# Moving the w2 load to another queue, and reordering norms, key finals and z sums in a linear-attention block

## Chip, cores and metric

The kernel runs on one core of one Trainium2 chip. The metric is the device time of one execution in microseconds (us). The profile is one execution; its span (239.8 us) is a little shorter than the timed runs, since it counts from the first to the last recorded instruction.

## What is computed

The input is x with 2048 rows (tokens) of 640 elements, in bf16. The reference, cut to what matters:

```python
xn  = (x - mean(x)) / sqrt(var(x) + 1e-5)              # per row
qkv = xn @ wqkv                                        # 640 -> 3 * 640, 32 heads of 20
phi = lambda t: where(t > 0, t + 1, exp(t)) + 1e-6
pq, pk = phi(q), phi(k)
kv  = sum over rows of pk^T v                          # per head, 20 x 20
z   = sum over rows of pk                              # per head, 20
o   = (pq @ kv) / (pq . z + 1e-6)
s   = o @ wo                                           # 640 -> 640
g   = silu(relu(xn @ w1) @ w2)                         # 640 -> 1728 -> 640
out = x + s * g
```

## The kernel before

The program is written as one list of operations. A small scheduler gives each engine its part of the list, in the order of the list, and puts semaphore waits in front of an operation for what it reads and overwrites. So an engine never overtakes in its own list, and neither does a queue of transfers: the order in the text is the order on each engine.

The 2048 tokens are 16 tiles of 128 (t), or four chunks of 512 (j). The stages follow each other on TensorE:

1. tiles 0 to 3: transposed on TensorE, keys K (L471);
2. chunks 0 to 3: H blocks (w1, 13 of 128 columns for each chunk, L546), Q blocks (L524) and the K of the other tiles, in the order of a plan;
3. the denominators, then G = xn^T pk (160 matmuls, L759);
4. for eight pairs of tiles: U = hT w2 (L811), between them kv (L774), W = kv wo (L788) and the output tiles s (L850).

VectorE computes the statistics of a tile (L394, L398), GpSimd its reciprocal root (L400, L402), VectorE the normed tile (L413). A DMA transpose (L462) makes it an operand for K, H and Q.

```python
def aggr(t):                                   # VectorE L398, then GpSimd L400, L402
    bn_aggr(mv[:, t], stats[:, t])             # DVE
    rsv[:, t] = mv[:, t, 1] + EPS_LN           # POOL
    rsy[:, t] = rsv[:, t] ** -0.5              # POOL

def LN_stats(t): bn(t, 0); bn(t, 1); aggr(t)   # bn: DVE L394

def LN_norm(t):                                # DVE L413
    xn[:, t, :] = (xin[:, t % XR, :] - mv[:, t, 0:1]) * rsy[:, t:t + 1]
    if t + XR < T: x_load(t + XR)

def K_mm(t, b, ...):                           # PE L471, 10 matmuls of 128x320
def K_exp(t, b), K_relu(t, b):                 # ACT L488
def K_fin(t):                                  # DVE L504, L506
    e_ = min(e_, 1.0) + 1e-6
    pk[:, t, :] = e_ + r_
    zpend.append(t)

def z_add():                                   # POOL L482
    t = zpend.pop(0)
    zacc = zacc + pk[:, t, :]                  # fp32 accumulator, 128x640

def Q_block(j, f):                             # PE L524, 5 matmuls of 128x512, a bank of a ring of six
    e_ = exp(ps[b])                            # ACT L531
    r_ = max(ps[b], 0) + 1e-6                  # DVE L532, waits for the exp
    pqT[:, f, schunk(j)] = min(e_, 1) + r_     # DVE L534

def H_block(j, f):                             # PE L546, 5 matmuls of 128x512, a bank of the same ring
    hT[:, f, schunk(j)] = relu(ps[b])          # ACT L550
```

The plan of the chunks. Chunk 0 has 13 H blocks; chunk 1 has ten Q blocks between them, chunks 2 and 3 five each. `kat` says after which step of the plan the keys of a tile follow, `lnat` after which its statistics.

```python
for j in range(J):
    for n, item in enumerate(plans[j]):
        Q_block(...) or H_block(...)
        if n in lnat[j]:
            t = lnat[j][n]
            LN_stats(t)
            if j == 0:
                K_fin(t - 4); LN_norm(t); xnT_dma(t); LN_norm(t - 4); xnT_dma(t - 4)
        if j > 0 and n - 1 in lnat[j]:
            LN_norm(lnat[j][n - 1]); xnT_dma(lnat[j][n - 1])
        if n in kat[j]:
            K_mm(t, 0); K_exp(t, 0); K_relu(t, 0); K_fin(t)
        if n >= 3 and zpend and len(zpend) > (1 if j < J - 1 else 0):
            z_add()
        ...
        if j == J - 1:                         # the last chunk
            if n == 2:  z_split()              # POOL
            if n == 8:  z_col()                # PE, DVE
            if n == 14: H_half(0); H_half(1); den()
```

The end of `den` and what follows it on SyncE's queue:

```python
    # den(): PE L651, then DVE L656 and the reciprocal L660
    for i in range(J):                         # L666: reciprocals, repeated 20 times, to scratch memory
        dma("SP", scr[...] <- rden[...], R=[("rden",)], W=[("scr", i)])
    for m in range(C):                         # L672: read back into the layout of pqT
        dma("SP", Rr[m] <- scr[P*m : P*(m+1), :], R=[("scr", i) for i in range(J)], W=[("Rr", m)], ...)

for a in range(2):                             # L742: w2 takes the place of w1, so it waits for the last w1 matmul
    dma("SP", w2_sb[...] <- B_w2[...], W=[("w2", a)], extra=[lastW1])
for u in range(2):                             # L746
    dma("SP", w2l[...] <- B_w2[NF*P:FF, :], W=[("w2l", u)], extra=[lastW1])
for c in range(VC):                            # L750: takes the place of the tiles of x
    dma("SP", wo_sb[:, c, :] <- A_wo[...], W=[("wo", c)], extra=[last_norm[0]])
for jx in range(4):                            # L883: x once more, for the last sum
    dma("SP", xre[...] <- x2[...], W=[("xre", jx)], extra=[lastG])

def divide(i):                                 # DVE L677, five of them for each chunk
    pqT[:, m, schunk(i)] *= Rr[m][:, schunk(i)]
```

U of a tile is four groups of 13 matmuls for a pair (L811). In the stage U the operations `kv_block` and `divide` follow the first group, the W blocks the groups of pair 1, the output tiles the groups from pair 2 on.

Of the kernel before, what the change touches and what calls it, by code (L numbers as in the profile page):

```python
# [214 lines left out]
def bass_recurrent_scan__linear_attn_block__dense_activation_relu__prompt_kernel(  # L215
# [9 lines left out]
    Bb, S, D = A_x.shape  # L225
# [3 lines left out]
    FF = B_w1.shape[1]  # L229
    P = 128  # L230
    T = S // P
    J = S // 512
    C = D // P
    NF = FF // P
# [102 lines left out]
    def x_load(t):  # L337
        sl = t % XR
        dma("SP", lambda eng: eng.dma_start(xin[:, sl, :], x2[tok(t), :]), W=[("xin", sl)])

    def w_load(dst, src, key, extra=(), E="SP"):
        dma(E, lambda eng: eng.dma_start(dst, src.rearrange("(c p) n -> p c n", p=P)), W=[key], extra=extra)

    KA = 3
    F1 = 7 * P
    x_load(0)
    x_load(1)
    w_load(wqk[:, 0:KA, D:2 * D], A_wqkv[0:KA * P, D:2 * D], ("wk", 0))
    x_load(2)
    w_load(wqk[:, KA:C, D:2 * D], A_wqkv[KA * P:D, D:2 * D], ("wk", 1))  # L350
    x_load(3)
    w_load(w1_sb[:, :, 0:F1], B_w1[:, 0:F1], ("w1", 0))
    for t in range(4, XR):
# [9 lines left out]
    sc.op("POOL", lambda eng: eng.memset(mhalf[:, :], -0.5), W=[("mhalf",)])  # L363
    sc.op("POOL", lambda eng: eng.memset(ones[:, :], 1.0), W=[("ones",)])
    sc.op("POOL", lambda eng: eng.memset(zacc[:, :], 0.0), W=[("zacc",)])
    NWARM = 28
    sc.group("PE", [(lambda eng: eng.matmul(ps[7][:, 0:P], lhsT=zero[:], rhs=zero[:], start=True, stop=True))
                    for _ in range(NWARM)], R=[("zero",)], W=[("ps", 7)])
    sc.allow_unread.add(("ps", 7))

    def build_consts():
        sc.op("POOL", lambda eng: eng.memset(mh[:, :, :], 1.0), W=[("mh",)])
# [19 lines left out]
    def bn(t, a):  # L392
        xv = xin[:, t % XR, :]
        sc.op("DVE", lambda eng: eng.bn_stats(stats[:, t, a, :], xv[:, HN * a:HN * (a + 1)]),  # L394
              R=[("xin", t % XR)], W=[("stats", t, a)])
# [16 lines left out]
    def LN_norm(t):  # L412
        last_norm[0] = sc.op("DVE", lambda eng: eng.tensor_scalar(  # L413
            out=xn[:, t, :], in0=xin[:, t % XR, :], scalar1=mv[:, t, 0:1], scalar2=rsy[:, t:t + 1],
            op0=ALU.subtract, op1=ALU.mult), R=[("xin", t % XR), ("mv", t), ("rsy", t)], W=[("xn", t)])
        if t + XR < T:
            x_load(t + XR)
# [6 lines left out]
    def mean_act(t, lo):  # L424
        junk = ek[:, t % NEK, 0, 0:D - lo]
        sc.op("ACT", lambda eng: eng.activation(out=junk, in_=xin[:, t % XR, lo:D], func=ACTF.Copy, scale=1.0 / D,
                                                accum_out=msum[:, t, 1:2]),
              R=[("xin", t % XR)], W=[("msum", t, 1), ("ek_e", t % NEK)])
        sc.allow_unread.add(("ek_e", t % NEK))

    def centre(t):
        if t == 0:
            sc.op("DVE", lambda eng: eng.tensor_scalar(
                out=xn[:, t, :], in0=xin[:, t, :], scalar1=msum[:, t, 0:1], scalar2=msum[:, t, 1:2],
                op0=ALU.subtract, op1=ALU.subtract), R=[("xin", t), ("msum", t, 0), ("msum", t, 1)], W=[("xn", t)])
        else:
            sc.op("DVE", lambda eng: eng.tensor_scalar(
                out=xn[:, t, :], in0=xin[:, t, :], scalar1=msum[:, t, 1:2], scalar2=None,
                op0=ALU.subtract), R=[("xin", t), ("msum", t, 1)], W=[("xn", t)])
# [10 lines left out]
    def xcT_copy(t, b, part):  # L450
        psb = ps[b + part].bitcast(bf)
        c0, c1 = (0, TS) if part == 0 else (TS, C)
        dst = xcT[:, c0:c1, tok(t)]
        src = psb[:, 0:P * (c1 - c0)].rearrange("p (c q) -> p c q", c=c1 - c0)
        if part == 0:
            sc.op("DVE", lambda eng: eng.tensor_copy(dst, src), R=[("ps", b)], W=[("xcT", t, 0)])
        else:
            sc.op("ACT", lambda eng: eng.activation(out=dst, in_=src, func=ACTF.Copy), R=[("ps", b + 1)],
                  W=[("xcT", t, 1)])

    def xnT_dma(t):
        dma("SP", lambda eng: eng.dma_start_transpose(xnT[:, :, tok(t)], xn[:, t, :]), R=[("xn", t)], W=[("xnT", t)])  # L462
# [3 lines left out]
    def K_mm(t, b, k0=0, k1=C, halves=(0, 1)):  # L466
        fns = []
        for a in halves:
            for k in range(k0, k1):
                lhs = xcT if t < 4 else xnT  # L470
                fns.append(lambda eng, a=a, k=k, lhs=lhs: eng.matmul(  # L471
                    ps[b + a][:, 0:HN], lhsT=lhs[:, k, tok(t)], rhs=wqk[:, k, D + HN * a:D + HN * (a + 1)],
                    start=(k == 0), stop=(k == C - 1)))
        Rx = [("xnT", t)] if t >= 4 else ([("xcT", t, 0)] if k0 < TS else []) + ([("xcT", t, 1)] if k1 > TS else [])
        Rw = ([("wk", 0)] if k0 < KA else []) + ([("wk", 1)] if k1 > KA else [])
        sc.group("PE", fns, R=Rx + Rw, W=[("ps", b + a) for a in halves])
# [23 lines left out]
    def K_fin(t):  # L500
        es = t % NEK
        e_ = ek[:, es, 0, :]
        r_ = ek[:, es, 1, :]
        sc.op("DVE", lambda eng: eng.tensor_scalar(out=e_, in0=e_, scalar1=1.0, scalar2=1e-6, op0=ALU.min, op1=ALU.add),  # L504
              R=[("ek_e", es)], W=[("ek_e", es)])
        sc.op("DVE", lambda eng: eng.tensor_tensor(out=pk[:, t, :], in0=e_, in1=r_, op=ALU.add),  # L506
              R=[("ek_e", es), ("ek_r", es)], W=[("pk", t)])
        zpend.append(t)
# [65 lines left out]
    mean_act(0, HN)  # L574
    half_mean_dve()
    centre(0)
    mean_act(1, 0)
    transposes(0, 0)
    xcT_copy(0, 0, 0)
    xcT_copy(0, 0, 1)  # L580
    centre(1)
    K_mm(0, 2, 0, TS)
    bn(0, 1)
    aggr(0)
    mean_act(2, 0)
    K_mm(0, 2, TS, KA)
    transposes(1, 6)
    xcT_copy(1, 6, 0)
    xcT_copy(1, 6, 1)
    centre(2)  # L590
    K_mm(0, 2, KA, C)
    mean_act(3, 0)
    K_mm(1, 4, 0, TS)
    K_mm(1, 4, TS, C, (0,))
    transposes(2, 0)
    bn(1, 0)
    xcT_copy(2, 0, 0)
    xcT_copy(2, 0, 1)
    K_mm(1, 4, TS, C, (1,))
    w_load(w1_sb[:, :, F1:FF], B_w1[:, F1:FF], ("w1", 1), E="ACT")  # L600
    K_exp(0, 2)
    K_relu(0, 2)
    centre(3)
    bn(1, 1)
    aggr(1)
    K_mm(2, 6, 0, TS)
# [86 lines left out]
            if ql:  # L693
                plans[j].append(("q",) + ql.pop(0))
    kat = [{5: 4, 7: 5, 9: 6, 11: 7}, {7: 8, 11: 9, 15: 10, 19: 11}, {6: 12, 9: 13, 12: 14, 15: 15}, {}]
    lnat = [{0: 4, 2: 5, 4: 6, 6: 7}, {0: 8, 4: 9, 8: 10, 12: 11}, {0: 12, 3: 13, 6: 14, 9: 15}, {}]
    for j in range(J):
        for n, item in enumerate(plans[j]):
            if item[0] == "q":
                Q_block(item[1], item[2])  # L700
            else:
                lastW1 = H_block(item[1], item[2])
            if n in lnat[j]:
                t = lnat[j][n]
                LN_stats(t)
                if j == 0:
                    K_fin(t - 4)
                    LN_norm(t)
                    xnT_dma(t)
                    LN_norm(t - 4)  # L710
                    xnT_dma(t - 4)
            if j > 0 and n - 1 in lnat[j]:
                t = lnat[j][n - 1]
                LN_norm(t)
                xnT_dma(t)
            if n in kat[j]:
                t = kat[j][n]
                K_mm(t, 0)
                K_exp(t, 0)
                K_relu(t, 0)  # L720
                K_fin(t)
            if n >= 3 and zpend and len(zpend) > (1 if j < J - 1 else 0):
                z_add()
            if j == 1 and n == 2:
                w_load(wv_sb[:, :, :], A_wqkv[:, 2 * D:3 * D], ("wv",))
            if j == 2 and n == 1:
                build_consts()
            if j == J - 1:
                while zpend:
                    z_add()  # L730
                if n == 2:
                    z_split()
                if n == 8:
                    z_col()
                if n == 14:
                    lastW1 = H_half(0)
                    lastW1 = H_half(1)
                    den()

    for a in range(2):  # L740
        c0, c1 = (0, 7) if a == 0 else (7, NF)
        dma("SP", lambda eng, c0=c0, c1=c1: eng.dma_start(  # L742
            w2_sb[:, c0:c1, :], B_w2[P * c0:P * c1, :].rearrange("(c p) n -> p c n", p=P)),
            W=[("w2", a)], extra=[lastW1])
    for u in range(2):
        dma("SP", lambda eng, u=u: eng.dma_start(w2l[64 * u:64 * (u + 1), :], B_w2[NF * P:FF, :]),  # L746
            W=[("w2l", u)], extra=[lastW1])
    for c in range(VC):
        r0 = VR * c if c < VC - 1 else D - P
        dma("SP", lambda eng, c=c, r0=r0: eng.dma_start(wo_sb[:, c, :], A_wo[r0:r0 + P, :]),  # L750
            W=[("wo", c)], extra=[last_norm[0]])

    def G_block(k, b):
# [208 lines left out]
```

## Time and profile before

The median of three timed runs is 240.54 us (240.16 to 243.49).

| engine | busy us | share of the span |
|---|---|---|
| TensorE, matmuls (PE) | 219.2 | 91% |
| TensorE, weight loads (PEld, beside the matmuls) | 134.0 | 56% |
| VectorE (DVE) | 112.5 | 47% |
| ScalarE (ACT) | 87.8 | 37% |
| GpSimd (POOL) | 45.0 | 19% |

The stretches of the old kernel, from the view of busy times by window:

| stretch, us | what | PE busy | DVE busy | POOL busy | DMA share, GB/s |
|---|---|---|---|---|---|
| 0 to 15.2 | loads, tiles 0 to 3 | 11.85 | 7.04 | 3.79 | 0.81, 267 |
| 15.2 to 37.5 | chunk 0 | 19.57 | 18.65 | 14.30 | 0.69, 169 |
| 37.5 to 67.8 | chunk 1 | 30.14 | 27.01 | 9.34 | 0.21, 50 |
| 67.8 to 94.0 | chunk 2 | 25.10 | 17.50 | 10.78 | 0.13, 26 |
| 94.0 to 117.1 | chunk 3, denominators | 22.84 | 10.20 | 3.49 | 0.00, 1 |
| 117.1 to 139.1 | G | 21.94 | 1.00 | 0.00 | 0.78, 212 |
| 139.1 to 148.6 | between G and U | 0.05 | 0.00 | 3.30 | 1.06, 359 |
| 148.6 to 239.8 | U, kv, W, s | 87.69 | 31.12 | 0.00 | 0.19, 64 |

How to read the profile: a line such as "L482" is a line of the kernel's source. A row of groups gives line, engine, operation, output<-input, the count, the busy time and the mean of one in ns. A row of waits reads "who waited <- for whom: us in total, times, the longest". A row of the timeline is start, length, engine, line, operation, count, and in brackets the idle time before it with what ended it; a row may merge several like instructions. In the page's slices each digit is the busy share of one fortieth of the span in tenths; PEclk is the clock that TensorE was granted.

### The profile page before, as it was taken

To read this page: it belongs to the slowest core of one execution; us is meant where nothing else is said; L and a number is where in the kernel's file an instruction comes from. 1 tells how busy PE (TensorE), PEld (TensorE's weight loads), DVE (VectorE), ACT (ScalarE), POOL (GpSimd) and SP (SyncE) were. 2 spreads that over 40 slices of the span, in tenths; PEclk is the share of its full clock that TensorE was granted. 3 is DMA by queue.
4 is the path that set the end of the run, shared out by engine and by line. 5 is a ranking of instruction groups with operands and counts; after the bars stand their busy time and mean duration, and the time that the engine had idled before them with its cause. 6 is when DMAs were issued, how large, how long until landed. Compare 5 with 4: busy or idle time off the path is not lost.

```text
span 239.8 us, 3474 instructions
## 1 busy us (share of the span) xinstructions
PE 219.2 (91%) x1425; PEld 134.0 (56%) x1436; DVE 112.5 (47%) x211; ACT 87.8 (37%) x144; POOL 45.0 (19%) x69
## 2 busy tenths in 40 slices
PE   6899969999999989999999912999999999999994
PEld 5554434555545544444577701767776776777672
DVE  3388995999847981560600000482132432224143
ACT  5496635566655655554212130023202110210211
POOL 2154673333241365200000050000000000000000
PEclk9999999999999999999999995799999999999998
DMA  6998740511101120000099799920010101000011
GB/s 190 353 296 178 165 113 12 164 29 27 31 0 27 30 52 3 0 0 3 15 211 211 262 386 338 363 79 0 3 55 27 57 27 55 30 27 29 28 55 56
DMA packets 26992, 23.90 MB, mean 100 GB/s; under 512 B 11744, under 2 KB 26336, under 8 KB 26976
## 3 DMA queue, kind: packets, MB, share of 16 engines
q1 hardware_dynamic: 25664, 21.80, 31.2%
q10 hardware_dynamic: 1312, 1.88, 2.4%
q8 instruction: 11, 0.18, 0.3%
q14 instruction: 5, 0.04, 0.1%
HBM read 15.81 MB, written 5.24 MB: 88 GB/s over the span
## 4 chain that ended last, share of the span: by engine, by line
PE 64%; DMA 14%; DVE 13%; SPq 3%; POOL 2%; issue 2%; ACT 1%; DVEq 0%
PE psT L811 25%; PE psT L546 13%; PE psT L850 8%; PE psT L524 8%; PE psT L471 6%; DMA reg<-in_B_w_dram 5%; DMA scr<-regE 4%; DVE reg L413 3%; DVE stats L394 3%; DMA reg<-reg 2%; DMA reg<-in_A_wqkv_dram 2%; POOL rsy L402 2%; DVE pqT L534 2%; SPq L666 1%; DVE regE L660 1%
## 5 line engine op out<-in xcount | busy, mean ns | idle before, releaser
L811 PE MATMUL psT<-reg,hT 128*128 128x320 bf16 x416 | 62.2, 304 | 9.5 <-DMA reg<-in_B_w_dram 9.5
L811 PEld LDWEIGHTS psT<-reg,hT 128*128 128x128 bf16 x416 | 40.8, 99 | 27.1 <-issue 10.9
L546 PE MATMUL psT<-reg 128*128 128x512 bf16 x191 | 45.5, 379 | 0.3 <-issue 0.2
L550 ACT ACTIVATE hT<-psT 128x512 bf16<-128x512 f32 x52 | 30.9, 600 | 18.3 <-PE psT L546 18.3
L864 DVE TENSOR_TENSOR reg<-psT,reg 128x640 bf16<-128x640 f32 (+1 forms) x17 | 13.3, 785 | 48.8 <-PE psT L850 47.6
L546 PEld LDWEIGHTS psT<-reg 128*128 128x128 bf16 x195 | 19.0, 98 | 22.1 <-ACT hTl L567 0.4
L482 POOL TENSOR_TENSOR zacc<-zacc,reg 128x640 f32<-128x640 f32 x16 | 23.0, 1435 | 7.9 <-DVE reg L506 7.6
L850 PE MATMUL psT<-reg,pqT 128*128 128x320 bf16 x160 | 24.3, 299 | 0.0
L524 PE MATMUL psT<-reg 128*128 128x512 bf16 x95 | 23.8, 379 | 0.3
L839 ACT ACTIVATE reg<-psT 128x640 bf16<-128x640 f32 x12 | 8.2, 702 | 43.1 <-PE psT L811 23.6
L759 PE MATMUL psT<-reg 128*128 128x320 bf16 x160 | 21.9, 299 | 0.0
L471 PE MATMUL psT<-reg 128*128 128x320 bf16 x120 | 18.3, 299 | 3.6 <-DMA reg<-reg 2.9
L488 ACT ACTIVATE regE<-psT 128x640 bf16<-128x640 f32 x24 | 15.6, 701 | 13.4 <-PE psT L471 13.4
L759 PEld LDWEIGHTS psT<-reg 128*128 128x128 bf16 x160 | 15.7, 98 | 6.2
L850 PEld LDWEIGHTS psT<-reg,pqT 128*128 128x128 bf16 x160 | 15.7, 98 | 6.1
L532 DVE TENSOR_SCALAR regE<-psT 128x512 bf16<-128x512 f32 x20 | 13.6, 680 | 11.3 <-ACT regE L531 11.3
L413 DVE TENSOR_SCALAR reg<-reg,mv,rsy 128x640 bf16<-128x640 bf16 x16 | 16.5, 1051 | 3.3 <-POOL rsy L402 3.3
L777 DVE TENSOR_TENSOR reg<-psT,mv 128x120 bf16<-128x120 f32 (+1 forms) x6 | 1.5, 268 | 34.8 <-PE psT L774 34.8
L471 PEld LDWEIGHTS psT<-reg 128*128 128x128 bf16 x120 | 11.3, 97 | 11.2 <-ACT hT L550 3.0
L839 ACT ACTIVATE reg<-psT,rsy 128x640 bf16<-128x640 f32 x4 | 3.2, 794 | 35.3 <-PE psT L829 30.1
L524 PEld LDWEIGHTS psT<-reg 128*128 128x128 bf16 x100 | 9.7, 98 | 11.4
L534 DVE SCALAR_TENSOR_TENSOR pqT<-regE 128x512 bf16<-128x512 bf16 x20 | 15.3, 766 | 0.7
(68 smaller groups left out, 175.8 us busy)
## 6 DMA issues: line engine op xcount, KB each, us to landing
reg<-in_A_x_dram SPq DMA_DIRECT2D x16, 160.0 KB, 2.8
scr<-regE SPq DMA_DIRECT2D x4, 640.0 KB, 8.7
reg<-in_A_x_dram SPq DMA_DIRECT2D x4, 640.0 KB, 10.6
out_dram<-reg SPq DMA_DIRECT2D x15, 160.0 KB, 1.8
reg<-in_B_w_dram SPq DMA_DIRECT2D x2, 1120.0 KB, 9.1
regE<-scr SPq DMA_DIRECT2D x4, 512.0 KB, 5.2
reg<-in_B_w_dram ACTq DMA_DIRECT2D x1, 1040.0 KB, 5.2
reg<-in_B_w_dram SPq DMA_DIRECT2D x1, 960.0 KB, 13.2
```

Of the source, the lines that this page charges most:

```text
L413: last_norm[0] = sc.op("DVE", lambda eng: eng.tensor_scalar(out=xn[:, t, :], in0=xin[:, t % XR, :], scalar1=mv[:, t, 0:1], scalar2=rsy[:, ...
L471: fns.append(lambda eng, a=a, k=k, lhs=lhs: eng.matmul(ps[b + a][:, 0:HN], lhsT=lhs[:, k, tok(t)], rhs=wqk[:, k, D + HN * a:D + HN * (a + 1)],
L482: sc.op("POOL", lambda eng: eng.tensor_tensor(out=zacc[:, :], in0=zacc[:, :], in1=pk[:, t, :], op=ALU.add), R=[("zacc",), ("pk", t)], W=[( ...
L488: sc.op("ACT", lambda eng: eng.activation(out=o_.rearrange("p (a n) -> p a n", a=2), in_=ps2(b, HN), func=func, scale=scale), R=[("ps", b) ...
L524: sc.group("PE", [(lambda eng, k=k: eng.matmul(ps[b], lhsT=wqk[:, k, P * f:P * (f + 1)], rhs=xnT[:, k, schunk(j)], start=(k == 0), stop=(k ...
L532: sc.op("DVE", lambda eng: eng.tensor_scalar(out=r_, in0=ps[b], scalar1=0.0, scalar2=1e-6, op0=ALU.max, op1=ALU.add), R=[("ps", b), ("er_e ...
L534: sc.op("DVE", lambda eng: eng.scalar_tensor_tensor(out=pqT[:, f, schunk(j)], in0=e_, scalar=1.0, in1=r_, op0=ALU.min, op1=ALU.add), R=[(" ...
L546: a = sc.group("PE", [(lambda eng, k=k: eng.matmul(ps[b], lhsT=w1_sb[:, k, P * f:P * (f + 1)], rhs=src[:, k, :], start=(k == 0), stop=(k = ...
L550: sc.op("ACT", lambda eng: eng.activation(out=hT[:, f, schunk(j)], in_=ps[b], func=ACTF.Relu), R=[("ps", b)], W=[("hT", j, f)])
L759: fns.append(lambda eng, t=t, a=a: eng.matmul(ps[b + a][:, 0:HN], lhsT=xn[:, t, P * k:P * (k + 1)], rhs=pk[:, t, HN * a:HN * (a + 1)], sta ...
L811: sc.group("PE", [(lambda eng, f=f: eng.matmul(ps[b][:, 0:HN], lhsT=hT[:, f, tok(t)], rhs=w2_sb[:, f, HN * n:HN * (n + 1)], start=(f == 0 ...
L850: sc.group("PE", [(lambda eng, c=c, a=a: eng.matmul(ps[b + a][:, 0:HN], lhsT=pqT[:, c, tok(t)], rhs=wf[:, c, HN * a:HN * (a + 1)], start=( ...
```

## The change

Five things are altered, in the order of the program.

1. The first loads: the key weights wk come ahead of the second tile of x, in pieces of two and three blocks (KA = 2 where it was 3). The warm-up matmuls of zeros are 32 where they were 28, six more stand behind the first transposes, and the sums, centrings and statistics of tiles 0 to 3 take other places in the list. It is to start the first keys sooner.
2. Chunk 0: the statistics and norms of tiles 4 to 7 come at steps 0 to 3, ahead of the finals of the keys of tiles 0 to 3; the norms and transposes of tiles 0 to 3 come after them. It is to have the transposed tiles ready for K.
3. In chunks 1 and 2 the norms come closer together. The z adds begin at a late step of each chunk (`zfrom`): none in chunk 0, from step 10 in chunk 1, from step 8 in chunk 2. It is to keep GpSimd's adds apart from the norms on VectorE.
4. Chunk 3: wo is loaded at its first step, z_split, z_col and the denominators come at steps 1, 6 and 11 where they came at 2, 8 and 14.
5. w2 is loaded from ScalarE's queue, where it stood on SyncE's behind the writes and reads of scr. It is to arrive before U needs it.

The diff:

```diff
--- before.py
+++ after.py
@@ -341,13 +341,13 @@
     def w_load(dst, src, key, extra=(), E="SP"):
         dma(E, lambda eng: eng.dma_start(dst, src.rearrange("(c p) n -> p c n", p=P)), W=[key], extra=extra)
 
-    KA = 3
+    KA = 2
     F1 = 7 * P
     x_load(0)
+    w_load(wqk[:, 0:KA, D:2 * D], A_wqkv[0:KA * P, D:2 * D], ("wk", 0))
     x_load(1)
-    w_load(wqk[:, 0:KA, D:2 * D], A_wqkv[0:KA * P, D:2 * D], ("wk", 0))
+    w_load(wqk[:, KA:C, D:2 * D], A_wqkv[KA * P:D, D:2 * D], ("wk", 1))
     x_load(2)
-    w_load(wqk[:, KA:C, D:2 * D], A_wqkv[KA * P:D, D:2 * D], ("wk", 1))
     x_load(3)
     w_load(w1_sb[:, :, 0:F1], B_w1[:, 0:F1], ("w1", 0))
     for t in range(4, XR):
@@ -363,10 +363,13 @@
     sc.op("POOL", lambda eng: eng.memset(mhalf[:, :], -0.5), W=[("mhalf",)])
     sc.op("POOL", lambda eng: eng.memset(ones[:, :], 1.0), W=[("ones",)])
     sc.op("POOL", lambda eng: eng.memset(zacc[:, :], 0.0), W=[("zacc",)])
-    NWARM = 28
-    sc.group("PE", [(lambda eng: eng.matmul(ps[7][:, 0:P], lhsT=zero[:], rhs=zero[:], start=True, stop=True))
-                    for _ in range(NWARM)], R=[("zero",)], W=[("ps", 7)])
+
+    def fill(n):
+        sc.group("PE", [(lambda eng: eng.matmul(ps[7][:, 0:P], lhsT=zero[:], rhs=zero[:], start=True, stop=True))
+                        for _ in range(n)], R=[("zero",)], W=[("ps", 7)])
+
     sc.allow_unread.add(("ps", 7))
+    fill(32)
 
     def build_consts():
         sc.op("POOL", lambda eng: eng.memset(mh[:, :, :], 1.0), W=[("mh",)])
@@ -574,33 +577,33 @@
     mean_act(0, HN)
     half_mean_dve()
     centre(0)
-    mean_act(1, 0)
     transposes(0, 0)
     xcT_copy(0, 0, 0)
     xcT_copy(0, 0, 1)
-    centre(1)
-    K_mm(0, 2, 0, TS)
+    mean_act(1, 0)
+    fill(6)
     bn(0, 1)
     aggr(0)
-    mean_act(2, 0)
-    K_mm(0, 2, TS, KA)
+    centre(1)
+    K_mm(0, 2, 0, KA)
     transposes(1, 6)
     xcT_copy(1, 6, 0)
     xcT_copy(1, 6, 1)
+    K_mm(0, 2, KA, C)
+    mean_act(2, 0)
     centre(2)
-    K_mm(0, 2, KA, C)
-    mean_act(3, 0)
     K_mm(1, 4, 0, TS)
     K_mm(1, 4, TS, C, (0,))
     transposes(2, 0)
-    bn(1, 0)
     xcT_copy(2, 0, 0)
     xcT_copy(2, 0, 1)
     K_mm(1, 4, TS, C, (1,))
+    mean_act(3, 0)
+    centre(3)
     w_load(w1_sb[:, :, F1:FF], B_w1[:, F1:FF], ("w1", 1), E="ACT")
     K_exp(0, 2)
     K_relu(0, 2)
-    centre(3)
+    bn(1, 0)
     bn(1, 1)
     aggr(1)
     K_mm(2, 6, 0, TS)
@@ -693,7 +696,8 @@
             if ql:
                 plans[j].append(("q",) + ql.pop(0))
     kat = [{5: 4, 7: 5, 9: 6, 11: 7}, {7: 8, 11: 9, 15: 10, 19: 11}, {6: 12, 9: 13, 12: 14, 15: 15}, {}]
-    lnat = [{0: 4, 2: 5, 4: 6, 6: 7}, {0: 8, 4: 9, 8: 10, 12: 11}, {0: 12, 3: 13, 6: 14, 9: 15}, {}]
+    lnat = [{0: 4, 1: 5, 2: 6, 3: 7}, {0: 8, 3: 9, 6: 10, 9: 11}, {0: 12, 2: 13, 4: 14, 6: 15}, {}]
+    zfrom = [99, 10, 8, 0]
     for j in range(J):
         for n, item in enumerate(plans[j]):
             if item[0] == "q":
@@ -704,11 +708,15 @@
                 t = lnat[j][n]
                 LN_stats(t)
                 if j == 0:
-                    K_fin(t - 4)
+                    if n >= 2:
+                        K_fin(2 * n - 4)
+                        K_fin(2 * n - 3)
                     LN_norm(t)
                     xnT_dma(t)
-                    LN_norm(t - 4)
-                    xnT_dma(t - 4)
+            if j == 0 and 4 <= n < 8:
+                LN_norm(n - 4)
+            if j == 0 and 8 <= n < 12:
+                xnT_dma(n - 8)
             if j > 0 and n - 1 in lnat[j]:
                 t = lnat[j][n - 1]
                 LN_norm(t)
@@ -719,37 +727,37 @@
                 K_exp(t, 0)
                 K_relu(t, 0)
                 K_fin(t)
-            if n >= 3 and zpend and len(zpend) > (1 if j < J - 1 else 0):
+            if n >= zfrom[j] and zpend and j < J - 1:
                 z_add()
             if j == 1 and n == 2:
                 w_load(wv_sb[:, :, :], A_wqkv[:, 2 * D:3 * D], ("wv",))
             if j == 2 and n == 1:
                 build_consts()
+            if j == J - 1 and n == 0:
+                for c in range(VC):
+                    r0 = VR * c if c < VC - 1 else D - P
+                    dma("SP", lambda eng, c=c, r0=r0: eng.dma_start(wo_sb[:, c, :], A_wo[r0:r0 + P, :]),
+                        W=[("wo", c)], extra=[last_norm[0]])
             if j == J - 1:
                 while zpend:
                     z_add()
-                if n == 2:
+                if n == 1:
                     z_split()
-                if n == 8:
+                if n == 6:
                     z_col()
-                if n == 14:
+                if n == 11:
                     lastW1 = H_half(0)
                     lastW1 = H_half(1)
                     den()
 
     for a in range(2):
         c0, c1 = (0, 7) if a == 0 else (7, NF)
-        dma("SP", lambda eng, c0=c0, c1=c1: eng.dma_start(
+        dma("ACT", lambda eng, c0=c0, c1=c1: eng.dma_start(
             w2_sb[:, c0:c1, :], B_w2[P * c0:P * c1, :].rearrange("(c p) n -> p c n", p=P)),
             W=[("w2", a)], extra=[lastW1])
     for u in range(2):
-        dma("SP", lambda eng, u=u: eng.dma_start(w2l[64 * u:64 * (u + 1), :], B_w2[NF * P:FF, :]),
+        dma("ACT", lambda eng, u=u: eng.dma_start(w2l[64 * u:64 * (u + 1), :], B_w2[NF * P:FF, :]),
             W=[("w2l", u)], extra=[lastW1])
-    for c in range(VC):
-        r0 = VR * c if c < VC - 1 else D - P
-        dma("SP", lambda eng, c=c, r0=r0: eng.dma_start(wo_sb[:, c, :], A_wo[r0:r0 + P, :]),
-            W=[("wo", c)], extra=[last_norm[0]])
-
 
 
     def G_block(k, b):
```

## The prediction

> **What bounds the kernel now.** I read four views in this order: the page's forty slices, the list of waits, the chain of work between 117 and 150 us, and the timeline of single instructions where VectorE and GpSimd meet. In the slices, one slice is 6.0 us:
>
> ```profile
> PE   6899969999999989999999912999999999999994
> PEclk9999999999999999999999995799999999999998
> DMA  6998740511101120000099799920010101000011
> ```
>
> TensorE is at nine tenths nearly everywhere. It has one deep hole, in slices 23 and 24 (138 to 150 us), and the granted clock falls there, to 5 and 7 tenths; small dips lie in slices 0, 1, 5 and 14. So the end is set by TensorE's work plus its holes, and the holes are what a reordering can win. The waits name the big one, and the small ones for the transposed blocks:
>
> ```profile
> ACT reg L839 <- PE psT L829: 49.5, 4, 19.0
> ...
> PE psT L811 <- DMA reg<-in_B_w_dram: 9.5, 1, 9.5
> ...
> PE psT L471 <- DMA reg<-reg: 2.9, 3, 2.3
> ```
>
> The first line is harmless (an engine with time to spare). The second is one wait of 9.5 us: the first matmul with w2. The chain, from the reciprocal on, shows why w2 is late (start, length, what):
>
> ```profile
> 114.74 3.36 DVE regE L660
> ...
> 121.77 10.71 DMA scr<-regE
> ...
> 132.49 0.34 SPq L672
> ...
> 134.82 0.45 SPq L742
> 135.27 0.04 issue
> 135.31 13.15 DMA reg<-in_B_w_dram
> 148.46 0.09 issue
> 148.55 1.49 PE psT L811 x5
> ```
>
> SyncE issues in program order. The four writes of the reciprocals to scr go out from 118.1; the reads back (L672) wait for them until 132.5; only behind these does SyncE reach w2 (L742). w2 needs nothing of scr: its only condition, the end of the last w1 matmul, was met at about 117.15, when the 160 matmuls of G begin. These end at 139.05; w2 lands at 148.5.
>
> The last view is of the lock. GpSimd's z add lasts 1.40 us, LN_norm on VectorE (L413) 0.44 alone. Where they meet, the timeline has:
>
> ```profile
> 24.28 2.87 POOL L482 TENSOR_TENSOR zacc<-zacc,reg 128x640 f32<-128x640 f32 x2
> 24.34 2.99 DVE L413 TENSOR_SCALAR reg<-reg,mv,rsy 128x640 bf16<-128x640 bf16 x2 [0.46 <-POOL rsy L402]
> ```
>
> Two norms take 2.99 us for 0.88. Each ends some 0.1 to 0.2 us after a z add has ended. The same is seen of L534 (80.53, 1.71 us for 0.69, ends 0.55 after the z add), and of L504 and L506 (1.51 and 1.62 for 0.27 and 0.49).
>
> **What the Trainium skill says.** "SBUF — State Buffer", section "SBUF: two separate sides": the port pair that VectorE and GpSimd share is an exclusive lock; an operation with two SBUF inputs, or in a two-port mode, waits for the whole GpSimd instruction. The trace agrees, as just shown, and L532, which reads PSUM, kept 0.69 us at 61.84 inside a z add. "DMA: Bandwidth & Descriptors", section "Queues, rings and completion order": each DMA engine takes turns between the queue rows by packets, so that w2 on ScalarE's queue isn't behind scr but beside it; section "Issuing engines are not separate DMA queues" adds that the sixteen engines are the same, so that no bandwidth is won. This trace shows a DMA share of 0.78 and 212 GB/s from 117.1 to 139.1, but no two large streams of both queues at that place. "TensorE: Matmul & The Clock Gate", section "What's actually happening": after an idle window of about 3.4 us the clock is halved until a busy window. The trace agrees: the thirteen first matmuls after the hole take 3.62 us, later ones 1.77.
>
> **The change part by part.**
>
> (1) w2 from ScalarE. Its issue moves from 134.8 to about 118.0, behind the last Relu (117.35 + 0.60). In flight then: scr, alone at 211 GB/s of the slices and occupying the engines for 13.7 us (118.8 to 132.5); and w2 with its rest, 2.3 MB, 6.2 us at the 370 GB/s that the windowed DMA view shows for such loads. The denominators also move from plan step 14 to 11, three H blocks of 1.08 us, so scr starts 3.2 us earlier against G. The engines' sum from 115.6: 13.7 + 6.2 = 19.9, to 135.5. w2 shares equally and ends before; even last it beats 139.05, by 3.5 us. The hole of 9.5 goes. So does the cold clock behind it: 3.62 − 1.77 = 1.85, and some 0.25 of the thirty matmuls of kv (L774, 1.90 in the chain). **Removed: 11.6 us.** What comes later by it: Rr's reads are issued at 135.5, and 2.6 MB at 370 need 7 us, so 143, beside xre perhaps 146; the divides (20 of 0.42 on VectorE, spaced 0.34, 6.7 us) end at 153. The first s_tile needs them 23.1 us into U less 2.1 for the clock: 139.05 + 21.0 = 160. Hidden. wo, moved to chunk 3, takes 0.96 MB (2.6 us) from the end of the DMA burst.
>
> (2) The first loads and fills. The key weights go second, in pieces of 2 and 3 blocks. The K matmuls at 6.84 waited 1.7 for them. About 1.0 of it comes back; the sums of tile 1 now stand behind the copies of tile 0 on ScalarE (5.15 + 0.49, then 0.72 + 0.19, then centre 0.38: transposes of tile 1 at 7.05 where they were at 8.39), but tile 3's wait for three such rounds, as before. K3 ends at about 14.8 where it was 15.2. The 6 fills (0.113 each) lie in idle time. **Removed: 0.4.**
>
> (3) Norms ahead of finals in chunk 0, no z add there. Chunk 0 took 15.25 to 37.5 = 22.25 us for 13 H of 1.08 and 4 K of 1.36 = 19.5: 2.8 idle. New norms of tiles 4 to 7 cost 0.88 + 0.21 + POOL's 0.9 + 0.44 = 2.4 each, back to back, with four finals of 0.76 between: tile 7 normed about 10.5 us into the chunk, transposed 2.7 later, 13.2; its K is at 11 × 1.08 + 3 × 1.36 + 1.08 = 17.0. No wait. The transposes of tiles 0 to 3 come last and may hold the first Q block by some tenths. **Removed: 2.5.**
>
> (4) z adds late. In chunk 1 twelve z adds stand behind the norm of tile 11, nine with their data ready: they run back to back. I go through it on the clock of the old trace. VectorE brings tile 11's statistics to 54.2, rsy follows at 55.1. From there VectorE has twelve operations that need the lock (one norm, five L534, three L504, three L506), and each waits for one z add: 12 × 1.40 and some 2.2 of VectorE's own data time between them, until 74.0. In the old trace the last final of the chunk ended at 66.6. Then statistics of tile 12 to 75.1, rsy behind the twelfth z add 76.3, Q's two operations to 76.5, norm to 76.95, transpose 2.65: K of tile 12 at 79.6, where it was 75.3. Tiles 13 to 15 would follow in time (transposed at 82.6, 85.5, 89.2; needed at 84.3, 88.9, 93.5), so the old waits of chunk 2 (0.2 + 0.65 + 0.3) vanish and its end goes from 93.9 to 97.0. **Added: 3.1 at most.** All waits stand in a row in this sum, and VectorE idles for ScalarE at L532 at times (11.3 in the run), in which a z add costs nothing. I choose two thirds: 2.0.
>
> (5) z_split, z_col and the denominators earlier: the z adds end with chunk 2, as they did; this moves only scr, counted in (1).
>
> Sum: 240.5 − 11.6 − 0.4 − 2.5 + 2.0 = **228.0 us**.
>
> **Rivals.** *w2 is hidden, but scr pays.* If the scr writes, in packets of about 1 KB from 32 partitions a piece, suffer more than by equal turns, Rr lands near 155, the divides end at 162 and hold the second W block's copy on VectorE and s_tile: a new hole of 2 to 6 us in U, total 230 to 234. For it: slices 20 to 24 are already full of DMA. Against it: 17 us of slack between Rr and s_tile. *w2 later than G.* A halved rate would make it land at 141: 2 us lost, 230. *The z burst doesn't hurt*, because the ring of six PSUM banks and three buffers for exponentials hide the lag: then 226. *It hurts in full*, and the banks of the late Q blocks hold H as well: 229 to 230. *The front gives nothing*, since the tile-by-tile chain ScalarE sum, VectorE centre, transpose stays: 0.4 lost.
>
> **Range and chances.** The removal of the hole is the firm term; nothing waits in its place short of 9 us. The terms (2) to (4) together lie between −4 and +1 against the middle of −0.9; a slower DMA phase may add 3. So 224.5 to 231.5. Two per cent are 4.8 us: to miss them more than half of 11.6 would have to return. Faster 0.95, same 0.04, slower 0.01.
>
> **What would show it.** The wait of L811 for in_B_w gone, and TensorE's clock full in all slices: step 1. w2 landing by 136, scr's last piece by 136, the first divide near 144: its sum. H beginning near 14.8: step 2. L471's waits for transposes gone before 38 and chunk 0 at 19.5 to 20 us: step 3. A wait of K at tile 12 of 2 to 4 us, and L534 at about 1.5 mean in chunk 1: step 4; if L534 stays near 0.8 and K doesn't wait, step 4 is wrong and the time is near 226. A wait of L850 or L788 for VectorE in U would make it wrong the other way.

## The result and the profile after

The changed kernel takes 232.76 us (median of 4 runs, 232.4 to 233.14); the kernel before took 241.1 us beside it (240.16 to 243.49). The ratio is 0.964, 95% interval 0.957 to 0.972. The gain of 8.3 us is two thirds of the 12.5 that were predicted, and the time lies above the stated range (224.5 to 231.5). The profiled spans are 239.8 and 230.7 us, 9.1 apart.

The slices of the page, now 5.8 us each:

```profile
PE   8779999999986799999999998999999999999993
PEclk9999999999999799999999999999999999999999
DMA  6996590711000225000059969900010110001011
```

The deep hole of slices 23 and 24 is gone. A new one is in slices 12 and 13 (69 to 81 us), with a clock of 7 tenths in slice 13: a wait in chunk 2 that the old kernel didn't have. From the list of waits, the row for w2 (9.5) is missing, and these are new or larger (who <- for whom: us, times, the longest):

```profile
ACT reg L772 <- issue: 7.3, 1, 7.3
...
PEld psT L474 <- DMA reg<-reg: 3.6, 1, 3.6
...
PE psT L474 <- DMA reg<-reg: 3.1, 1, 3.1
```

L474 is K_mm; in the old list its DMA wait was 2.9 in three pieces, in chunks 0 and 2. Now it is one piece. The timelines of both kernels, cut at the starts of stages (us; the last matmuls are the ten of the last output tile), show where the 9.1 us lie:

| from, to | before | after | difference | predicted |
|---|---|---|---|---|
| start, first H | 15.25 | 15.20 | −0.05 | −0.4 |
| first H, chunk 1 | 22.26 | 19.25 | −3.01 | −2.5 |
| chunk 1, first Q of chunk 3 | 57.46 | 61.80 | +4.34 | +2.0 |
| first Q of chunk 3, G | 22.18 | 22.17 | −0.01 | 0 |
| G, U | 31.40 | 22.90 | −8.50 | −9.5 |
| U, last matmuls | 86.22 | 84.26 | −1.96 | −2.1 |
| last matmuls, end | 5.03 | 5.12 | +0.09 | 0 |

Chunks 1 and 2 give 4.3 us back. The timeline from step 10 of chunk 1 on shows how (start, length, engine, line, operation, count; in brackets the wait before it):

```profile
51.60 18.06 POOL L485 TENSOR_TENSOR zacc<-zacc,reg 128x640 f32<-128x640 f32 x11
51.67 1.51 DVE L416 TENSOR_SCALAR reg<-reg,mv,rsy 128x640 bf16<-128x640 bf16 x1 [1.00 <-POOL rsy L405]
...
56.50 1.60 DVE L509 TENSOR_TENSOR reg<-regE 128x640 bf16<-128x640 bf16 x1
...
65.45 1.25 PE L549 MATMUL psT<-reg 128*128 128x512 bf16 x5 [0.53 <-DVE regE L535]
...
73.15 0.45 DVE L416 TENSOR_SCALAR reg<-reg,mv,rsy 128x640 bf16<-128x640 bf16 x1 [0.46 <-POOL rsy L405]
...
76.27 2.85 PE L474 MATMUL psT<-reg 128*128 128x320 bf16 x10 [3.09 <-DMA reg<-reg]
```

In the old kernel, a final's sum alone and the keys of tile 12:

```profile
55.29 0.49 DVE L506 TENSOR_TENSOR reg<-regE 128x640 bf16<-128x640 bf16 x1
...
75.32 1.52 PE L471 MATMUL psT<-reg 128*128 128x320 bf16 x10
```

Eleven z adds run in one piece of 18.06 us, 1.64 for each. Beside them the VectorE operations with the lock last 1.17 to 1.60 us where they take 0.27 to 0.69 alone: a final's sum 1.60 for 0.49, L537 (L534 in the old kernel) 1.17 to 1.21 for 0.69. VectorE falls behind, an H block waits 0.53 for its bank, tile 12 is normed at 73.15, and its keys wait 3.09 us for the transpose. Then the ten matmuls take 2.85 us; the same ten took 1.52 before.

### The profile page after: what moved, and what is told of

The parts are those of the page before. It is cut to its first block, busy times and chain, and to the rows that moved or that the text cites. A ratio compares the mean times of both kernels' runs of the same rounds, so it can differ in the third digit from the quotient of the medians.

```text
span 230.7 us, 3497 instructions
## 1 busy us (share of the span) xinstructions
PE 218.0 (95%) x1436; PEld 133.4 (58%) x1446; DVE 108.9 (47%) x211; ACT 87.8 (38%) x144; POOL 46.7 (20%) x69
## 4 chain that ended last, share of the span: by engine, by line
PE 73%; DVE 14%; POOL 3%; issue 3%; DMA 2%; ACT 2%; SPq 1%; DVEq 0%; POOLq 0%
PE psT L819 25%; PE psT L549 17%; PE psT L767 10%; PE psT L858 9%; PE psT L474 5%; PE psT L527 4%; DVE regE L535 3%; DVE pqT L537 2%; DMA reg<-in_A_wqkv_dram 2%; DVE regE L507 2%; DVE stats L397 2%; DVE reg L509 2%; POOL rsy L405 1%; DVE reg L416 1%; PE psT L796 1%
## 5 line engine op out<-in xcount | busy, mean ns | idle before, releaser
L819 PE MATMUL psT<-reg,hT 128*128 128x320 bf16 x416 | 60.5, 299 | 0.8 <-ACT reg L772 0.8
L819 PEld LDWEIGHTS psT<-reg,hT 128*128 128x128 bf16 x416 | 40.2, 98 | 17.5 <-ACT reg L772 1.1
L549 PEld LDWEIGHTS psT<-reg 128*128 128x128 bf16 x195 | 18.9, 98 | 22.9 <-DVE regE L535 1.0
L485 POOL TENSOR_TENSOR zacc<-zacc,reg 128x640 f32<-128x640 f32 x16 | 24.3, 1516 | 10.7 <-DVE reg L509 9.9
L474 PE MATMUL psT<-reg 128*128 128x320 bf16 x120 | 19.6, 313 | 3.1 <-DMA reg<-reg 3.1
L767 PE MATMUL psT<-reg 128*128 128x320 bf16 x160 | 22.1, 299 | 0.0
L767 PEld LDWEIGHTS psT<-reg 128*128 128x128 bf16 x160 | 15.6, 98 | 6.5 <-ACT reg L772 0.4
L474 PEld LDWEIGHTS psT<-reg 128*128 128x128 bf16 x120 | 12.1, 102 | 10.4 <-DMA reg<-reg 3.6
L537 DVE SCALAR_TENSOR_TENSOR pqT<-regE 128x512 bf16<-128x512 bf16 x20 | 17.3, 864 | 0.7
L527 PEld LDWEIGHTS psT<-reg 128*128 128x128 bf16 x100 | 9.8, 99 | 11.9 <-issue 0.4
L534 ACT ACTIVATE regE<-psT 128x512 bf16<-128x512 f32 x20 | 11.9, 597 | 9.2 <-PE psT L527 9.1
L549 PE MATMUL psT<-regX,reg 128*128 128x512 bf16 x63 | 14.4, 379 | 0.9 <-ACT regE L491 0.9
L397 DVE BATCH_NORM_STATS2 stats<-reg 128x6 f32<-128x320 bf16 x32 | 14.1, 479 | 2.1 <-DMA reg<-in_A_x_dram 2.1
```

Source lines behind the costliest of these rows:

```text
L474: fns.append(lambda eng, a=a, k=k, lhs=lhs: eng.matmul(ps[b + a][:, 0:HN], lhsT=lhs[:, k, tok(t)], rhs=wqk[:, k, D + HN * a:D + HN * (a + 1)],
L485: sc.op("POOL", lambda eng: eng.tensor_tensor(out=zacc[:, :], in0=zacc[:, :], in1=pk[:, t, :], op=ALU.add), R=[("zacc",), ("pk", t)], W=[( ...
L527: sc.group("PE", [(lambda eng, k=k: eng.matmul(ps[b], lhsT=wqk[:, k, P * f:P * (f + 1)], rhs=xnT[:, k, schunk(j)], start=(k == 0), stop=(k ...
L537: sc.op("DVE", lambda eng: eng.scalar_tensor_tensor(out=pqT[:, f, schunk(j)], in0=e_, scalar=1.0, in1=r_, op0=ALU.min, op1=ALU.add), R=[(" ...
L549: a = sc.group("PE", [(lambda eng, k=k: eng.matmul(ps[b], lhsT=w1_sb[:, k, P * f:P * (f + 1)], rhs=src[:, k, :], start=(k == 0), stop=(k = ...
L767: fns.append(lambda eng, t=t, a=a: eng.matmul(ps[b + a][:, 0:HN], lhsT=xn[:, t, P * k:P * (k + 1)], rhs=pk[:, t, HN * a:HN * (a + 1)], sta ...
```

## The experiments

**w2 alone.** The old kernel with this edit and nothing else:

```diff
-        dma("SP", lambda eng, c0=c0, c1=c1: eng.dma_start(   # w2
+        dma("ACT", lambda eng, c0=c0, c1=c1: eng.dma_start(
-        dma("SP", lambda eng, u=u: eng.dma_start(w2l[...], ...
+        dma("ACT", lambda eng, u=u: eng.dma_start(w2l[...], ...
```

> The kernel before with one part of the change alone: w2 and its rest are issued from ScalarE's queue. Theory: the w2 part is worth what the two traces show between the start of G and the end (8.7 us of the wait and 2.0 of the cold clock), so 241.1 - 10.6 = 230.5 us, faster than the whole change, and U begins some 22.7 us after G. Rival (the parts depend on each other, so that w2 from ScalarE needs the earlier denominators and the earlier wo to be hidden): scr begins only 1 us ahead of w2, both end later than G, a wait of L811 for w2 of 1 to 4 us remains, and the time is 232 to 235 us.

Measured: 230.29 us (229.51 to 231.06), ratio 0.954 (0.949 to 0.960). From its timeline, TensorE at the end of G:

```profile
139.99 1.94 PE L811 MATMUL psT<-reg,hT 128*128 128x320 bf16 x13 [0.80 <-ACT reg L764]
```

U starts 22.7 us after G, with no wait for w2 and at the full clock. The part needs none of the others, although scr here begins 0.8 us after w2's first issue and its reads wait until 134.7. The rival falls. And w2 alone is 2.5 us faster than the whole change (230.29 against 232.76, measured at different times, each beside the old kernel at 241.1; in the profiled spans 1.4, 229.3 against 230.7): beside w2 on its own queue, the rest of the change costs time.

**All but w2.** The same edit, undone in the changed kernel.

> The changed kernel with w2 and its rest back on SyncE's queue, behind the writes and reads of scr: all parts of the change but the w2 part. Theory: the other parts together lose 2.5 us against the kernel with w2 alone on ScalarE (232.8 against 230.3), but the denominators, three H blocks earlier, now shorten the w2 hole from 9.5 to about 6.3 us; so 241.1 + 2.5 - 3.2 = 240.4 us, the same as before. Rival (the other parts are worth something in themselves, and lose only beside the ScalarE queue, by what its issue of 7.4 us holds up): 238 us or less.

Measured: 239.81 us (238.19 to 242.35) against 241.02; ratio 0.996 (0.992 to 0.999). The timeline has the old hole, shorter, and the slow matmuls behind it:

```profile
145.67 3.62 PE L819 MATMUL psT<-reg,hT 128*128 128x320 bf16 x13 [6.70 <-DMA reg<-in_B_w_dram]
```

9.51 went to 6.70, because the denominators and scr come earlier (scr's writes are issued at 114.81, in the old kernel at 118.12). So that reordering is worth 2.8 us only while w2 stands behind scr; with w2 on its own queue U waits for neither, whether scr comes early (the change) or late (w2 alone). The rival (238 or less) falls; the lowest run is 238.19. Tile 12 waits here as in the change, but this time at the full clock:

```profile
76.50 1.53 PE L474 MATMUL psT<-reg 128*128 128x320 bf16 x10 [3.08 <-DMA reg<-reg]
```

**No z add in chunk 1.** The sixteen adds start in chunk 2 and end in chunk 3.

```diff
-    zfrom = [99, 10, 8, 0]
+    zfrom = [99, 99, 8, 0]
-                if n == 6:
+                if n == 10:
                     z_col()
```

> The changed kernel, but no z add in chunk 1: all sixteen begin at step 8 of chunk 2 and end in chunk 3, and z_col comes at step 10. Theory (the lock: each z add of chunk 1 holds one operation of VectorE, so that tile 12 is normed late): the 3.1 us wait of the keys of tile 12 goes, the slow clock after it and the 0.5 us bank wait go too, 4.3 us less, so 228.5 us. Rival (the closer norms of chunk 1 and 2 overload VectorE by themselves): the wait of tile 12 stays at 2 to 3 us and the time stays within 1 us of 232.8. Second rival: the sixteen adds hold the Q finals of chunk 3 and so the denominators; TensorE waits at L638 or L651 in chunk 3 and half of the gain is lost, 230.5 us.

Measured: 234.06 us (233.57 to 234.74), 1.3 above the change. The wait of tile 12 is nevertheless gone: its keys start at 72.75 with 0.21 of waiting for the transpose, where they waited 3.09. The norms of chunks 1 and 2 stand as close as in the change, so it isn't they that make VectorE late, but the adds. The time went elsewhere, as the second rival said and by more (the first line from the waits, the second from GpSimd's timeline):

```profile
PE psT L641 <- POOL regE L636: 4.0, 1, 4.0
```
```profile
77.47 25.90 POOL L485 TENSOR_TENSOR zacc<-zacc,reg 128x640 f32<-128x640 f32 x16
```

Sixteen adds in a row take 25.90 us, and TensorE waits 4.0 for z_split at z_col, with a clock of 5 and 8 tenths in the two slices there. A run of adds has a length; moving it moves what waits for it.

**Matmuls of zeros in the wait.** They go to a free bank ahead of tile 12's keys, which then overwrite them.

```diff
+                if t == 12:
+                    sc.group("PE", [(lambda eng: eng.matmul(ps[0][:, 0:P], lhsT=zero[:], rhs=zero[:], ...))
+                                    for _ in range(40)], R=[("zero",)], W=[("ps", 0)])
                 K_mm(t, 0)
```

> The changed kernel with 40 more matmuls of zeros, 128 columns each, ahead of the keys of tile 12, in a bank that nothing else uses then; they fill some 2.2 us of the 3.1 us that TensorE waits there. Theory: the wait costs twice, by itself (3.1 us, which stays) and by the halved clock after it (about 2 us), so the time falls by 1.5 to 2 us to about 231 us and the ten matmuls of tile 12 take 1.5 us where they took 2.85. Rival (the slow matmuls after the wait come from something else, such as late weights): no change, 232.8 us.

Measured: 231.45 us (231.06 to 231.63), 1.3 less than the change; the span is 229.3, 1.4 less. TensorE's timeline:

```profile
72.96 2.40 PE L727 MATMUL psT<-zero 128*128 128x128 bf16 x40
76.21 1.53 PE L474 MATMUL psT<-reg 128*128 128x320 bf16 x10 [0.86 <-DMA reg<-reg]
```

The keys start at the same moment (76.21, in the change 76.27) but take 1.53 us instead of 2.85, and G begins 1.6 us sooner (116.78, 118.42). The rival (late weights) falls. In the change the wait is paid twice: by its length, and by the clock after it.

**The z adds spread.** Five in chunk 0 behind the norm of tile 3, five in chunk 1, six in chunk 2.

```diff
-    zfrom = [99, 10, 8, 0]
+    zfrom = [8, 10, 8, 0]
+    zmax = [5, 5, 99, 0]
-            if n >= zfrom[j] and zpend and j < J - 1:
-                z_add()
+            if n >= zfrom[j] and zpend and j < J - 1 and zmax[j] > 0:
+                zmax[j] -= 1
+                z_add(extra=[last_norm[0]])     # also waits for the last norm in the list
```

> The changed kernel with the sixteen z adds laid where VectorE has time: five in chunk 0 behind the norm of tile 3, five in chunk 1 from step 10, six in chunk 2 from step 8. Theory (the lag of VectorE is about 0.6 us for each z add in the burst, and some 3.7 us of lag are hidden): with five adds tile 12 is normed in time, the wait of its keys, the bank wait and the slow clock go, 4.3 us less: 228.5 us. Rival (it is the norms set closer that make the lag, the adds only a part): a wait of 1 us or more stays at tile 12, and 230 to 231.5 us. The five in chunk 0 could hold the finals of tiles 6 and 7 by 1 us; no wait of TensorE is expected of that.

Measured: 226.98 us (226.71 to 227.23), ratio 0.944 (0.939 to 0.950). The page, and GpSimd's timeline:

```profile
PE   8869999999999999999999998999999999999993
```
```profile
27.94 7.58 POOL L485 TENSOR_TENSOR zacc<-zacc,reg 128x640 f32<-128x640 f32 x5 [2.96 <-DVE reg L416]
...
52.60 8.09 POOL L485 TENSOR_TENSOR zacc<-zacc,reg 128x640 f32<-128x640 f32 x5 [0.56 <-DVE reg L416]
```

No digit of TensorE below 9 is left between slice 3 and the one at the start of U. G starts at 113.26, 5.2 us before that of the change. I had expected 4.3: I took it from the comparison with the old kernel, whose chunk 2 had waits of its own (some 1.3), and those went too. The rival falls: the norms are as close as before, and tile 12 doesn't wait. And chunk 0 takes 19.25 us with five adds behind its norms, as it does in the change without any. So what chunk 0 won there came from the order of norms and finals; taking the adds out of it wasn't needed.

**The fifth block of G in other banks.** U's new first wait, 0.80 us, is for ScalarE to empty bank 0. In the change:

```profile
140.56 0.70 ACT L772 ACTIVATE reg<-psT 128x640 bf16<-128x640 f32 x1 [3.64 <-PE psT L767]
...
141.32 1.94 PE L819 MATMUL psT<-reg,hT 128*128 128x320 bf16 x13 [0.80 <-ACT reg L772]
```

```diff
-        lastG = G_block(k, (0, 2)[k % 2])
+        lastG = G_block(k, (0, 2, 0, 2, 4)[k])
```

> The changed kernel, but the fifth block of G goes to PSUM banks 4 and 5 instead of 0 and 1. Theory: with w2 there in time, the first matmul of U waits 0.8 us for ScalarE to empty bank 0 of the fifth G block; with other banks this wait goes: 0.8 us less, 232.0 us. Rival: U waits for something else at that point (w2 landing, the Silu table), and the time stays at 232.8 us.

Measured: 232.42 us (230.97 to 233.77), no difference that this spread can hold. The spread goes with the clock: the two runs with a mean clock of 0.990 and 0.992 took 232.97 and 233.77 us, which is no gain against the change (232.4 to 233.14 at 0.990 to 0.992), and the two with 0.997 and 0.999 took 231.88 and 230.97. The profile is of one of the latter, in which tile 12 waits but keeps the full clock:

```profile
76.83 1.53 PE L474 MATMUL psT<-reg 128*128 128x320 bf16 x10 [3.09 <-DMA reg<-reg]
```

The theory was half right. The wait at bank 0 is gone, and another has its place (from the waits):

```profile
PE psT L782 <- DVE reg L785: 1.0, 1, 1.0
```

L782 is kv. Its last two blocks want banks that VectorE must empty, and VectorE waits for GpSimd to zero kvp, which takes 3.30 us from the end of G.

**Earlier statistics of tile 1.** This kernel was run once, for its profile.

```diff
     mean_act(3, 0)
+    bn(1, 0)
+    bn(1, 1)
+    aggr(1)
     centre(3)
...
     K_relu(0, 2)
-    bn(1, 0)
-    bn(1, 1)
-    aggr(1)
```

> The changed kernel with the statistics of tile 1 ahead of the centring of tile 3. Theory (H starts at 15.2 us as before although the keys end sooner, since ScalarE's exp of tile 1 waits for the reciprocal root of tile 1, whose statistics the change moved behind that centring): H begins at about 14.4 us, 0.7 to 0.8 sooner. Rival (H waits for the w1 load or for ScalarE's sums): it stays at 15.2.

TensorE's first H in the change, with the exp of tile 1 that it waits for, and then in this kernel:

```profile
13.44 4.21 ACT L491 ACTIVATE regE<-psT,rsy 128x640 bf16<-128x640 f32 x6 [0.71 <-POOL rsy L405]
...
15.20 2.97 PE L549 MATMUL psT<-regX,reg 128*128 128x512 bf16 x13 [0.88 <-ACT regE L491]
```
```profile
14.53 2.75 PE L549 MATMUL psT<-regX,reg 128*128 128x512 bf16 x12
```

H starts 0.67 us sooner; the rival falls. Its start varies: it is 14.89 to 15.58 in the six traces that begin as the change does, and 14.36 to 14.53 in the three with the earlier statistics. The one time, 232.57 us, can't show the gain: tile 12's keys are held by VectorE in this kernel too (a wait of 3.10, with the slow clock behind it), and G starts at 118.21, where it started at 118.42 in the change.

**The three together, and the last wait.** First the spread, the banks and the statistics:

> The spread z adds, the fifth block of G in banks 4 and 5, and the statistics of tile 1 ahead of the centring of tile 3. If the three add up: 228.5 - 0.8 (U's first wait) - 0.7 (H starts sooner) = 227.0 us. Rival: an earlier H start is taken back by the transposes or x loads, 227.7 us.

Measured: 226.88 us (226.51 to 227.09), span 224.7, where the spread alone had 226.98 and 225.5: 0.1 less in the medians, 0.8 in the spans. The expected 227.0 was met by luck, since it started from 228.5, and the spread alone had already come to 226.98. G starts 0.85 sooner; the wait at kv (1.0) replaces that at bank 0, as it did in the kernel with the banks alone. Then its cause:

```diff
-    sc.op("POOL", lambda eng: eng.memset(kvp, 0.0), W=[("kvz",)], extra=[lastG])
+    sc.op("DVE", lambda eng: eng.memset(kvp, 0.0), W=[("kvz",)], extra=[lastG])
```

> The kernel with spread adds, banks 4 and 5 for the fifth block of G and early statistics of tile 1, and besides the zeroing of kvp behind G on VectorE instead of GpSimd. In that kernel and in the one with the banks alone, the wait of U for bank 0 (0.8 us) gave way to a wait of the last kv matmuls for VectorE (1.0 us), which waits for GpSimd's memset of 3.3 us. Theory: on VectorE the memset ends in time, neither wait is left, 1.0 us less: a span of 223.7 us and a time of 225.9 us. Rival: VectorE needs 2 us or more for it, and the divides behind it hold the first W copies: no gain, 226.9 us.

Measured: 225.73 us (224.88 to 226.18), ratio to the old kernel 0.935 (0.930 to 0.940), span 223.7. VectorE's and TensorE's timelines behind G:

```profile
135.24 1.66 DVE L891 MEMSET reg<- 128x1920 uint32 x1 [25.03 <-PE psT L769]
```
```profile
134.61 1.93 PE L821 MATMUL psT<-reg,hT 128*128 128x320 bf16 x13
136.38 1.59 PE L784 MATMUL psT<-reg,wv_sb 128*128 128x120 bf16 x30
137.82 5.46 PE L821 MATMUL psT<-reg,hT 128*128 128x320 bf16 x39
```

Half as long on VectorE, and no wait from G through kv to U. This is the fastest version found, 7.0 us under the change; its span and its median say the same (1.0 and 1.15 under the version before it, which was measured at another time).

## Why the prediction was wrong

It failed mainly in step (4), the cost of the late z adds, and a little in (1) and (2). The mechanisms it named were all there. Two things in step (4) failed: the discount to two thirds, and a term that was left out, the slow clock behind the wait that it foresaw.

- **(4), added 2.0, measured 4.34.** The chain worked out by hand was close. It put the end of the last final of chunk 1 at 74.0 on the old clock, 70.9 when shifted by the 3.06 won until then; it ended at 70.4. It put tile 12's keys at 79.6, shifted 76.5; they began at 76.27. What failed first is the sentence "I choose two thirds: 2.0". The discount had no ground: in the timeline of the burst, 51.6 to 70 us, VectorE waits for ScalarE nowhere, and in that part of the old kernel it waited only 0.21 and 0.28 at L532; most of the 11.3 lay elsewhere. The rest is an omission. Step (1) charges a hole with the slow clock behind it, step (4) doesn't, though it foresaw a TensorE wait of that order. From tile 12's keys to chunk 3 the old kernel took 19.65 us with some 1.3 of waits; the new one took 19.98 without those waits, with 1.6 of slow clock, as the matmuls of zeros showed. So: 4.0 late at tile 12, plus 1.6, less 1.3. In the trace of the kernel with w2 back, whose wait at tile 12 kept the full clock, the same stretch from chunk 1 to chunk 3 costs 2.76 against the old kernel: under the 3.1 of the chain, over the 2.0. One sign that step (4) named came out smaller: L537 has a mean of 0.88 us between 34.4 and 64.7 us (chunk 1), and 1.17 to 1.21 in the burst, where about 1.5 was expected.
- **(1), removed 11.6, measured 10.5** (8.50 and 1.96). w2 landed in time and scr's reads started at 135.1 where 135.5 stood; the divides began at 145.1 where it said near 144. "Nothing waits in its place short of 9 us" was wrong by 0.80: ScalarE's copy of the fifth block out of bank 0 had ended 0.7 us after G in the old kernel too, hidden in the hole. G itself took 0.2 longer (22.10 for 21.90). The clock term held: 1.96 for 2.1. Its 1.85 sets a length (3.62) against a distance of starts (1.77); starts against starts give 1.65 for U (3.42 less 1.77) and 0.31 for kv, which is the 1.96.
- **(2), removed 0.4, measured 0.05,** which is nothing: H starts between 14.89 and 15.58 in the traces that begin as the change does. The keys of tile 3 ended sooner, but H needs a bank that the exp of tile 1 empties, and the change moved tile 1's statistics back. The step looked at loads and transposes only.
- **(3), removed 2.5, measured 3.01.** No wait of K for a transpose is left in chunk 0, and the first Q waited some 0.3.
- **(5), nothing: held**, and the wo move cost nothing that shows.

Of the rivals, "it hurts in full" came nearest, at 229 to 230 us; the slow clock and bank 0 bring it from there to about 231.5. The 4.8 us between 228.0 and 232.76 are 3.4 of gain that didn't come in the span, 0.6 from the start of the sum (240.5, where the old kernel took 241.1 beside the change), and 0.8 between the gain in span (9.1) and in the medians (8.3). The last is the choice of executions: the two that were profiled took 241.52 and 232.40 us themselves, 9.1 apart.

## What to carry to other kernels

A transfer that waits for nothing may still stand behind one that does: look in each issuing queue for a transfer whose own condition was met long before its issue. When a hole is closed, ask what ended inside it, for that is the next wait; and ask of a TensorE wait of about 3 us whether the slow clock comes after it, for those that a change brings as well as those it removes: here that was 1.6 us, in some executions and not in others. A GpSimd add of 1.40 us held a locked VectorE operation until it lasted 1.17 to 1.60 us, so lay such work where VectorE has slack and not in one run ahead of something that TensorE needs.

## What the runs showed of the hardware

The issue of the same four w2 transfers on ScalarE took 2.7 us in all where it came first (w2 alone: 0.99 and 1.70), and 7.9 us in the change, where scr's writes were already under way (7.9 to 8.4 in the kernels made from it that leave w2 there). No run separates that order from what else differs. In the change's ScalarE timeline:

```profile
118.63 2.23 ACTq L755 DMA_DIRECT2D reg<-in_B_w_dram  x2
120.89 5.62 ACTq L759 DMA_DIRECT2D reg<-in_B_w_dram  x2
126.55 1.47 ACT L772 ACTIVATE reg<-psT 128x640 bf16<-128x640 f32 x2 [7.33 <-issue]
```

ScalarE copies nothing meanwhile; G had two pairs of banks to live on, and lost 0.2 us in the change and 0.54 in the kernel with other banks (a wait before its third block). I hadn't counted this.

A wait of about 3.1 us at tile 12 was followed by the slow clock in two traces (3.09 in the change, 3.10 with the earlier statistics of tile 1: the ten matmuls took 2.85 and 2.58 us) and by the full clock in two others (3.08 with w2 back, 3.09 with other banks: 1.53 each). What decides between them stays open. Both slow ones are shorter than the idle window of about 3.4 us for which the prediction names the Trainium skill ("TensorE: Matmul & The Clock Gate", section "What's actually happening"); here the measurement decides. A wait of 0.86 us, and the old kernel's 2.30 in chunk 0, had the full clock behind them; 4.0, 6.70 and 9.51 us had the slow one.
